# The first 30 microseconds of a gated dilated convolution: who writes the zeros, when the second x is asked for, and the order of the first octet

## The chip, the cores and the metric

The kernel runs on one core of a Trainium2 chip. The metric is device time in microseconds (us), as the median of a few runs. Beside it stands one profiled execution, from which all rows below are taken; the profile names the engines PE (TensorE matmul), PEld (TensorE weight load), DVE (VectorE), ACT (ScalarE), POOL (GpSimd) and SP (SyncE). A name with a q behind it (SPq, ACTq) is the engine's own sequencer, on which it issues DMAs.

## The reference

```
B, T, D, K = 2, 16000, 144, 15          # all bf16; x (B,T,D), w (K,D,2D), w_o (D,D)
xp = pad(x, 28 rows of zeros ahead of each sequence)
h  = sum over i of  xp[:, 28-2i : 28-2i+T, :] @ w[i]       # a causal convolution, dilation 2
z  = tanh(h[..., :D]) * sigmoid(h[..., D:])
return z @ w_o
```

So each output row needs 15 input rows two apart, each times a 144x288 matrix, then a gate and a 144x144 product.

## The kernel before

**Tiling.** Each of the two sequences is cut into 8 windows of 2048 rows with 32 rows ahead (16 windows in all). Within a window the rows are taken by their index modulo 16: one matmul has 128 rows, 16 apart, as its stationary operand. The 8 even or 8 odd residues of a window form an *octet*; there are 32 octets. The convolution is not computed tap by tap. The 15 taps are combined by sums of weights and differences of inputs in the manner of a fast filter algorithm, so that each octet needs fewer products. The sums of weights are made once, on VectorE (`sm`, `ss`, `a1v`, `av`, `ev`, part of `bc`) and on TensorE by products with an identity (`raw_sums`, `pair_sums`, into `bcv` and `bc`; ScalarE copies them out). The differences of x (`d2`, `d4`, `d8`, `d28`, `d24`, `d48`, `d248`) are made by VectorE for each window.

**The 128 + 16 split of the channels.** The 144 channels are 128 plus 16. The 128 come in by a transposing DMA straight from x (`xn`, line 89). The other 16 take a detour. `gather` loads them to `xt` (line 99; 104 partitions of 22 pieces of 32 bytes). ScalarE copies them by residue (`rest`, line 113), VectorE forms a difference (`rest_diff`, line 117), and `spread` (line 123) writes both halves, of 104x4 pieces of 160 bytes each, to a DRAM scratch `xg`. `remainder` (line 128) then reads `xg` back by transposing DMAs, as `rx` (first half) and `re` (second half). Rows of `xg` that lie ahead of a sequence, or past its end, are written with zeros or with rows of x (lines 217 to 229).

**The order of the work.** All engines but GpSimd are scheduled by hand: instructions run on each engine in the order in which the program issues them. Each DMA takes one of a few semaphores in turn and waits until the last user of that semaphore has landed. SP's queue holds the loads of x and of w, the raw remainder weights (lines 205, 206), `rx`, `re`, then the next window's `xt` and `xn`, and so on. From the first octet on, the order comes from `PLAN` (line 16), a list of named steps, each with an offset in octets; they are sorted into `todo` (line 556) and issued one by one (line 568). Pieces of the first octet's preparation are put before a named step by `late` (line 301).

**The named steps.** An octet has leaves A1, A2, A3, B, C, E. `v` is a leaf's common matmuls, `k` a ScalarE copy of that bank, `p` its private matmuls, `d` a ScalarE duplicate of a bank, `B2`, `B3`, `C2` direct matmuls with `d24` and `re`. `q`, `t3` and `y` are VectorE combinations that read those banks and so free them. A2 and A3 need `rx`; B2, B3, C2 and E need `re`. `xl` loads a window's x, `xt` its 16 other channels, `cr` and `dr` are `rest` and `rest_diff`, `wg` is `spread`. There are five PSUM banks for B, C and E, two for A and one (`po`) for the output product.

**Ahead of it all**, 20 matmuls of zeros (128x512, line 186) run on TensorE while the first loads come in.

**Out-projection weights.** `wo_z`, `wo_m` and `wo_bd` hold w_o in shifted copies (lines 248 to 259): 16 loads for `wo_z`, one for `wo_m`, 8 for `wo_bd`, all issued by GpSimd. `wo_z` is first used by the output product of octet 0 (line 440), three octets later; the other two serve only the last octet.

Of the kernel before, what the change touches and what calls it, by code (L numbers as in the profile page):

```python
# [8 lines left out]
BF16 = mybir.dt.bfloat16  # L9
F32 = mybir.dt.float32  # L10
# [16 lines left out]
def kernel(  # L27
# [14 lines left out]
    nc = tc.nc  # L42
    P = 128
    NWARM = 20
    MANUAL = {mybir.EngineType.PE, mybir.EngineType.Activation, mybir.EngineType.DVE, mybir.EngineType.SP}
    B, T, D = x.shape
    K = w.shape[0]
    D2 = w.shape[2]
    assert D2 == 2 * D and w.shape[1] == D and D == 144 and K == 15
    CM = 128  # L50
    CR = D - CM
    NG = 8
    H = 32
    WT = 16 * P
    WB = H + WT
    NJ = WB // 4 + 8
# [3 lines left out]
    wins = []  # L60
# [55 lines left out]

        nc.vector.tensor_tensor(out=sets[wi]["xs"][:, 1], in0=by_residue(wi, 2), in1=by_residue(wi, 0), op=ALU.subtract)

    def spread(wi, eng=nc.sync):

        for q in (0, 1):
            dst = bass.AP(xg.tensor, xg[wi, q, H // 4 * (wins[wi][1] == 0), 0:1].offset, [[5 * CR, NX], [NJ * CR, 4], [1, 5 * CR]])
            eng.dma_start(out=dst, in_=sets[wi]["xs"][:, q].rearrange("p r j c -> p r (j c)"))

# [41 lines left out]
    def add(o, a, b_, eng=None):  # L166
        (eng or nc.vector).tensor_tensor(out=o, in0=a, in1=b_, op=ALU.add)
# [34 lines left out]
    nc.gpsimd.memset(raw[96:P, 1, :], 0.0)  # L202
    for c in range(0, 16, 4):
        nc.sync.dma_start(out=w_all[:, c:min(c + 4, K), :], in_=w[c:min(c + 4, K), 0:CM, :].rearrange("k c d -> c k d"))  # L204
    nc.sync.dma_start(out=raw[:, 0, :], in_=w[0:K:2, CM:D, :])
    nc.sync.dma_start(out=raw[0:P - CR, 1, :], in_=w[1:K:2, CM:D, :])


    swap = const.tile([P, P], BF16)
    nc.gpsimd.memset(swap[:], 0.0)  # L210
# [1 line left out]
                            compare_op=ALU.not_equal, fill=1.0, base=CR - P, pattern=[[CR, NG], [-1, CR]], channel_multiplier=1)  # L212
    ident = const.tile([P, P], BF16)
    make_identity(nc, ident[:])


    nc.scalar.dma_start(out=xg[:].rearrange("w q n c -> (w q) (n c)")[:, 4 * NJ * CR:], in_=zero[0:2 * NW, 0:CR * CR])
    for wi in [i for i in range(NW) if wins[i][1] == 0]:
        def ahead_of(q, r, n, j, rows):
            return bass.AP(xg.tensor, xg[wi, q, r * NJ + j, 0:1].offset, [[NJ * CR, n], [1, rows * CR]])  # L220
        eng = nc.gpsimd if wi else nc.scalar
        eng.dma_start(out=ahead_of(0, 0, 4, 0, H // 4), in_=zero[0:4, 0:H // 4 * CR])
        eng.dma_start(out=ahead_of(1, 0, 2, 0, H // 4), in_=zero[0:2, 0:H // 4 * CR])
        eng.dma_start(out=ahead_of(1, 2, 2, 0, H // 4 - 1), in_=zero[0:2, 0:H // 4 * CR - CR])
        eng.dma_start(out=ahead_of(1, 2, 2, H // 4 - 1, 1), in_=x[wins[wi][0], 0:2, CM:D])
    for lo, e in [(i + 1, i + NW // B) for i in range(0, NW, NW // B)]:
        for q in (0, 1):
            dst = bass.AP(xg.tensor, xg[lo, q, WB // 4, 0:1].offset, [[2 * (4 * NJ + 16) * CR, e - lo], [NJ * CR, 4], [1, H // 4 * CR]])
            nc.gpsimd.dma_start(out=dst, in_=zero[0:4 * (e - lo), 0:H // 4 * CR])
    rest(0)  # L230

    s_r = const.tile([P, D2], BF16)
# [2 lines left out]
    def summed(parts, outs):  # L235

        t = bank(False)
        for i, (l, r) in enumerate(parts):
            nc.tensor.matmul(t[:, 0:D2], lhsT=l, rhs=r, start=i == 0, stop=i == len(parts) - 1)
        for o, sign in outs:  # L240
            nc.scalar.mul(out=o, in_=t[:, 0:D2], mul=sign)

    def rest_sums(which):
        even, odd = ((swap[:], raw[:, k, :]) for k in (0, 1))
        for parts, outs in (([even, odd], [(s_r[:], 1.0), (ns_r[:], -1.0)]), ([odd], [(wo_p[:], 1.0)]), ([even], [(we_r[:], 1.0)]))[which]:
            summed(parts, outs)

    nc.gpsimd.dma_start(out=wo_m[:], in_=w_o[0:CM, :])

    nc.gpsimd.memset(wo_z[:], 0.0)  # L250
    for g in range(9):
        if g:
            nc.gpsimd.dma_start(out=wo_z[0:CR * g, g, 0, :], in_=w_o[D - CR * g:D, :])
        if g < 8:
            nc.gpsimd.dma_start(out=wo_z[CR * g:P, g, 1, :], in_=w_o[0:P - CR * g, :])

    nc.gpsimd.memset(wo_bd[:], 0.0)
    for g in range(NG):
        nc.gpsimd.dma_start(out=wo_bd[g * CR:(g + 1) * CR, g, :], in_=w_o[CM:D, :])
    pre0 = derive_steps(sets[0])  # L260
    for k in ("d8", "d4"):
        pre0[k]()
    rest_diff(0)
    spread(0, nc.scalar)
    remainder(0, 0)
    remainder(0, 1)

# [13 lines left out]
        if c == 2:  # L281
            pre0["d48"]()

    def raw_sums(j):
        for e in (1, 0):
            summed([(ident[:], w_all[:, 8 * j + 2 * i + e, :]) for i in range(4)], [(bcv[:, j, e], 1.0)])

    bc = const.tile([CM, 4, 2, D2], BF16, name="bc")

    def pair_sums(j):  # L290
        for i in (2 * j, 2 * j + 1):
            for e in (1, 0):
                summed([(ident[:], wq[:, i, k, e, :]) for k in (0, 1)], [(bc[:, i, e, :], 1.0)])

    raw_sums(0)
    pair_sums(0)
    add(av[:], quad[:, :, 0], quad[:, :, 1])
    pre0["d2"]()
    add(bc[:, 2:4], wq[:, 2:4, 0], wq[:, 2:4, 1])
    pre0["d28"]()  # L300
    late = [(0, {"pA1_0"}, lambda: rest_sums(slice(0, 3))), (0, {"pA2_0", "vB", "vC"}, lambda: raw_sums(1)), 
            (0, {"q2_0", "B2_0", "B2_1", "C2_0", "C2_1", "vE"}, lambda: pre0["d24"](slice(0, 1))),
            (0, {"q3_0", "B3_0", "B3_1", "vE"}, lambda: pre0["d24"](slice(1, 2))),
            (0, {"q3_0", "B3_0", "B3_1", "vE"}, lambda: add(ev[:], w_all[:, 0:16:8, :], w_all[:, 4:16:8, :])),
            (0, {"yB2_0", "pE_0"}, pre0["d248"])]

    def mm(ps, l, r, start, stop, on=False):
        nc.tensor.matmul(ps[:, 0:D2], lhsT=l, rhs=r, start=start, stop=stop, skip_group_check=on)  # L308

# [154 lines left out]
    def issue(n, name):  # L464
        wi, rho = octs[n]
        if name == "xl":
            sets[wi].update(load(wi))
            sets[wi].update(steps=derive_steps(sets[wi]))
            return
        s = sets[wi]  # L470
        if name in fetch:
            fetch[name](wi)
            return
        if name in s["steps"]:
            s["steps"][name]()
            return
        if n not in live:
            live[n] = Octet(s, rho)
            live[n].by_phase = n == NO - 1
        o = live[n]  # L480
        if name[0] in "vkpd" and name[1] in "ABCE":
            leaf = getattr(o, name[1:3] if name[1] == "A" else name[1] + "1")
            if name[0] == "v":
                leaf.common()
            elif name[0] == "k":
                leaf.copy()
            else:
                (leaf.private if name[0] == "p" else leaf.dup)(int(name[-1]))
        elif name[:2] == "t3":
            o.t3(int(name[-1]))  # L490
        elif name[:3] == "a1s":
            o.a1s(int(name[-1]))
        elif name[0] == "q":
            o.q(*((o.A2, "q2") if name[1] == "2" else (o.A3, "q3")), int(name[-1]),
                ALU.subtract if name[1] == "2" else ALU.add)
        elif name[0] in "BC":
            getattr(o, name[0:2])(int(name[-1]))
        elif name[0] == "y":
            leaf = {"B": o.B1, "C": o.C1, "E": o.E1}["E" if name[1:3] == "C3" else name[1]]
            ts, q = (leaf.other, "q3") if name[1:3] == "B3" else (leaf.ts, "t3" if name[1:3] == "C3" else "q2")  # L500
            k = (0 if name[1] == "B" else 1) + (2 if name[2] == "3" else 0)
            o.out_y(k, ts, q, ALU.subtract if name[1] == "B" else ALU.add, int(name[-1]))
        elif name[:2] == "th":
            o.act(int(name[2]), "th", 0, ACT.Tanh)
        elif name[:2] == "sg":
            o.act(int(name[2]), "sg", D, ACT.Sigmoid)
        elif name[0] == "m":
            for part in "ab" if o.by_phase else "z":
                o.mult(int(name[1]), part)
        elif name == "zt":  # L510
            o.zt = z_load(o.t["z"])
        elif name[0] == "g":
            outproj(o, int(name[1]))
        elif name[:2] == "po":
            project_out(o, window_out(n), int(name[2]))
        else:
            assert name == "ost"
            store(wi, nc.scalar)
# [16 lines left out]
    def finish():  # L535
# [11 lines left out]
        for g, by in ((0, "ACT"), (1, "DVE"), (2, "ACT")):  # L547
# [5 lines left out]
    even = set(pre0) | set(fetch) | {"xl"}  # L553
    outwards = {"g0", "g1", "g2", "po0", "po1", "po2", "ost"}
    at_wg = next((at, i) for i, (name, at) in enumerate(plan) if name == "wg")
    todo = sorted((2 + at_wg[0], False, at_wg[1] - .5, n, name) if n == 2 and name in ("cr", "dr") else
                  (n + at, n > 1 and n + at < 0, i, n, name) for i, (name, at) in enumerate(plan) for n in range(NO)
                  if not (name in even and (n % 2 or n == 0) or name == "ost" and n % 2 == 0
                          or name in outwards and n >= NO - 3 or name == "zt" and n == NO - 1))
    gates = [(NO - 1, "m1")]  # L560
    for *_, n, name in todo:
        for e in [e for e in late if n == e[0] and name in e[1]]:
            e[2]()
            late.remove(e)
        if (n, name) in gates:
            gates.clear()
            finish_early()
        issue(n, name)
# [29 lines left out]
```

## Time and profile before

| | us |
|---|---|
| median of 3 runs (335.77 to 337.07) | 336.16 |
| the profiled execution, its own time | 338.06 |
| its span, first to last instruction | 336.3 |
| end of the 20 matmuls of zeros | 7.2 |
| first matmul with x (leaf A1 of octet 0) | 11.48 |
| first matmul with `rx` | 18.39 |
| first matmul with `re` | 21.38 |
| start of TensorE's last wait in the front, and its end | 25.09, 27.58 |
| first output product (`po`) | 45.54 |
| last matmul | 331.05 |

The busy table gives each engine's busy time over the span; the chain of waits follows the end of the kernel back to what released each step; the timeline lists instructions in order of time, with the idle time ahead of them and its releaser in brackets; the table of stretches gives each engine's busy time in one microsecond, with TensorE's granted clock (1.00 is full speed) and what the DMA engines moved. From the start to landing, DMAs of POOL took between 2.7 and 5.9 us; for the DMAs of SP and ACT the trace has no landing time of their own, and it is read from the instruction that waited for them.

### The profile page before, as it was taken

The page shows a single profiled execution, that of the slowest core. Times are in us where ns is not written, and L with a number is a line of the kernel's source. Part 1 is how long each engine was busy: PE and PEld are TensorE (multiplying, and loading weights), DVE is VectorE, ACT ScalarE, POOL GpSimd, SP SyncE. Part 2 cuts the span into 40 slices and gives each one's busy share as a digit, 9 for nine tenths or more (in the row PEclk, how much of TensorE's full clock was granted, in tenths as well). Part 3 has the DMA queues.
Part 4 walks back from the last instruction along what each step waited for, and adds up shares of the span by engine and source line. Part 5 has one row for each costly group of instructions (what it writes and reads, how often), then busy time and mean ns, then how long its engine had stood idle before and what let it go on. Part 6 is the DMA issues. An engine that isn't in the chain of part 4 may idle for free.

```text
span 336.3 us, 7414 instructions
## 1 busy us (share of the span) xinstructions
PE 322.1 (96%) x2649; PEld 303.3 (90%) x2649; DVE 293.9 (87%) x664; ACT 241.6 (72%) x571; POOL 22.7 (7%) x49
## 2 busy tenths in 40 slices
PE   7597999999999999999999999999999999999993
PEld 2485999999999999999999999999999999999982
DVE  2848999999989999999989999998989999998683
ACT  2542778877777787777777787777777887777763
POOL 7980000000000000000000000000000000000000
PEclk9897999999999999999999999999999999999999
DMA  9996558495976859595996858596885949484313
GB/s 168 170 153 122 132 101 190 111 196 144 162 185 119 187 108 209 115 187 161 119 226 115 174 115 198 130 167 177 119 209 111 202 98 230 122 140 131 37 35 127
DMA packets 195282, 49.64 MB, mean 148 GB/s; under 512 B 190786, under 2 KB 193198, under 8 KB 195246
## 3 DMA queue, kind: packets, MB, share of 16 engines
q1 hardware_dynamic: 188894, 40.07, 65.0%
q10 hardware_dynamic: 5296, 8.67, 7.4%
q0 software_dynamic: 1056, 0.44, 0.6%
q8 instruction: 20, 0.33, 0.4%
q14 instruction: 16, 0.13, 0.1%
HBM read 2.82 MB, written 11.40 MB: 42 GB/s over the span
## 4 chain that ended last, share of the span: by engine, by line
PE 89%; DMA 5%; SPq 2%; DVE 1%; issue 1%; ACT 0%; DVEq 0%; ACTq 0%
PE bc L308 55%; PE a L308 25%; PE po L440 9%; DMA xn<-in_x_dram 2%; DMA w_all<-in_w_dram 2%; SPq L128 2%; DMA xg<-xs 1%; SPq L89 0%; DVE o L432 0%; DVE y L398 0%; DVE z L410 0%; PE bc L444 0%; SPq L204 0%; SPq L99 0%; PE bc L447 0%
## 5 line engine op out<-in xcount | busy, mean ns | idle before, releaser
L308 PEld LDWEIGHTS <-d 128*128 128x128 bf16 x1792 | 226.0, 145 | 10.7 <-issue 3.5
L308 PE MATMUL bc<-w_all,d 128*128 128x288 bf16 x832 | 140.6, 287 | 0.3 <-DVE t L393 0.3
L398 DVE TENSOR_TENSOR y<-q,bc 128x288 f32<-128x288 f32 x192 | 86.5, 451 | 8.0 <-PE bc L308 6.0
L337 ACT COPY bc<-bc 128x288 f32<-128x288 f32 x97 | 38.5, 397 | 34.2 <-PE bc L308 29.1
L375 DVE TENSOR_TENSOR q<-a1s,a 128x288 f32<-128x288 f32 x126 | 54.3, 454 | 1.9 <-PE a L308 1.1
L430 ACT CAST o<-po 128x432 bf16<-128x432 f32 (+1 forms) x87 | 41.6, 478 | 17.0 <-PE po L440 17.0
L160 DVE TENSOR_TENSOR d<-d 128x516 bf16<-128x516 bf16 (+3 forms) x65 | 52.3, 806 | 0.0
L308 PE MATMUL a<-sm,d 128*128 128x288 bf16 x252 | 50.8, 289 | 0.0
L160 DVE TENSOR_TENSOR d<-xn 128x516 bf16<-128x516 bf16 (+2 forms) x48 | 41.3, 863 | 8.3 <-DMA xn<-in_x_dram 8.3
L337 ACT COPY a<-a 128x288 f32<-128x288 f32 x95 | 36.7, 386 | 12.2 <-PE a L308 9.0
L403 ACT ACTIVATE th<-y 128x576 bf16<-128x576 f32 x64 | 43.8, 684 | 1.1 <-DVE y L398 1.1
L403 ACT ACTIVATE sg<-y 128x576 bf16<-128x576 f32 x64 | 43.7, 682 | 0.0
L440 PE MATMUL po<-wo_z,zt 128*128 128x144 bf16 (+1 forms) x323 | 43.4, 253 | 0.0
L308 PE MATMUL bc<-bc,d 128*128 128x288 bf16 x256 | 41.8, 286 | 0.2 <-ACT bc L337 0.2
L308 PE MATMUL bc<-we_r,re 128*128 128x288 bf16 x128 | 36.9, 288 | 0.0
L308 PE MATMUL bc<-wo_p,re 128*128 128x288 bf16 x128 | 36.6, 286 | 0.0
L393 DVE TENSOR_TENSOR t<-q,bc 128x288 f32<-128x288 f32 x64 | 28.8, 451 | 8.3 <-PE bc L308 8.3
L440 PEld LDWEIGHTS <-zt 128*128 128x128 bf16 x341 | 29.9, 98 | 4.1
L341 ACT COPY bc<-bc 128x288 f32<-128x288 f32 x64 | 24.9, 391 | 11.7 <-PE bc L308 11.6
L398 DVE TENSOR_TENSOR y<-t,bc 128x288 f32<-128x288 f32 x64 | 26.3, 455 | 6.2 <-PE bc L308 6.2
L308 PEld LDWEIGHTS <-re 128*128 128x128 bf16 x256 | 28.9, 113 | 0.1
L410 DVE TENSOR_TENSOR z<-th,sg 128x576 bf16<-128x576 bf16 (+1 forms) x66 | 29.0, 442 | 0.0
(74 smaller groups left out, 270.2 us busy)
## 6 DMA issues: line engine op xcount, KB each, us to landing
out_dram<-o ACTq DMA_DIRECT2D x13, 576.0 KB
xg<-xs SPq DMA_DIRECT2D x30, 65.0 KB
xt<-in_x_dram SPq DMA_DIRECT2D x13, 71.5 KB
w_all<-in_w_dram SPq DMA_DIRECT2D x3, 288.0 KB
out_dram<-o SPq DMA_DIRECT2D x1, 576.0 KB
zt<-z SPq DMA_TRANSPOSE x31
out_dram<-o ACTq DMA_DIRECT2D x1, 468.0 KB
out_dram<-o ACTq DMA_DIRECT2D x1, 288.0 KB
```

The lines of the kernel that those rows point to most:

```text
L128: nc.sync.dma_start_transpose(out=t[:], in_=bass.AP(xg.tensor, xg[wi, q, 0:1, 0:1].offset, [[CR, 4 * NJ], [1, P]]))
L160: nc.vector.tensor_tensor(out=o, in0=a, in1=b_, op=ALU.subtract)
L308: nc.tensor.matmul(ps[:, 0:D2], lhsT=l, rhs=r, start=start, stop=stop, skip_group_check=on)
L337: nc.scalar.copy(out=self.ts[1][:, 0:D2], in_=self.ts[0][:, 0:D2])
L341: nc.scalar.copy(out=self.other[i][:, 0:D2], in_=self.ts[i][:, 0:D2])
L375: nc.vector.tensor_tensor(out=self.get(cp_pool, name, [P, 2, D2], F32)[:, i, :], in0=self.t["a1s"][:, i, :], in1=leaf.ts[i][:, 0:D2], op=op)
L393: nc.vector.tensor_tensor(out=self.get(cp_pool, "t3", [P, 2, D2], F32)[:, i, :], in0=self.t["q3"][:, i, :], in1=self.C1.ts[i][:, 0:D2], op ...
L398: nc.vector.tensor_tensor(out=y[:, k + 4 * i, :], in0=self.t[q][:, i, :], in1=ts[i][:, 0:D2], op=op)
L403: nc.scalar.activation(out=t[:], in_=self.t["y"][:, k::2, lo:lo + D], func=func)
L410: nc.vector.tensor_tensor(out=o, in0=th[:, :, lo:lo + n], in1=sg[:, :, lo:lo + n], op=ALU.mult)
L430: nc.scalar.copy(out=o, in_=a)
L440: nc.tensor.matmul(o.po[g][:, (a - r0) * D:(e - r0) * D], lhsT=o.zt[:, c, :], rhs=wo_z[:, c, a - c + 1:e - c + 1, :].rearrange("p r e -> p ...
```

## The change

In words, in the order of the program:

- The two raw remainder loads (lines 205, 206) are issued by SP behind the second of the four loads of w instead of behind the fourth.
- The zeros at the end of `xg`, and those of window 0, are issued by GpSimd instead of ScalarE. Those of the other windows are issued behind window 0's spread, by GpSimd as before.
- Window 0's spread is split: the first half is issued by ScalarE, the second by GpSimd (`engines` in `spread`).
- The out-projection weights are cleared and loaded later: `weights_out` is called behind the sum `ev`, and a one-element copy of `ev` on GpSimd (`held`) holds the loads until that sum is done. `wo_m` comes behind `wo_z`.
- `rest_sums` (four matmuls with `raw`) runs behind `raw_sums(0)`, ahead of the pair sums; `raw_sums(1)` is split in two, one half ahead of octet 0's first step and one behind it.
- `keep(n)` issues n matmuls of zeros (128x512) into the `po` bank: 5, 1 and 2 at three places of the front.
- The load of the second window's x (`xl` of octet 2) is issued on SP right behind `re`, ahead of that window's `xt`.
- Octet 0's steps up to `yB2_0` and `d248` are listed in `first`; what is listed is left out of `todo`'s run. `late` is gone.
- GpSimd joins the engines scheduled by hand.

```diff
-    MANUAL = {mybir.EngineType.PE, mybir.EngineType.Activation, mybir.EngineType.DVE, mybir.EngineType.SP}
+    MANUAL = {mybir.EngineType.PE, mybir.EngineType.Activation, mybir.EngineType.DVE, mybir.EngineType.SP, mybir.EngineType.Pool}
...
-    def spread(wi, eng=nc.sync):
+    def spread(wi, engines=(nc.sync, nc.sync)):
-        for q in (0, 1):
+        for q, eng in enumerate(engines):
...
     for c in range(0, 16, 4):
         nc.sync.dma_start(out=w_all[:, c:min(c + 4, K), :], in_=w[c:min(c + 4, K), 0:CM, :].rearrange("k c d -> c k d"))
-    nc.sync.dma_start(out=raw[:, 0, :], in_=w[0:K:2, CM:D, :])
-    nc.sync.dma_start(out=raw[0:P - CR, 1, :], in_=w[1:K:2, CM:D, :])
+        if c == 4:
+            nc.sync.dma_start(out=raw[:, 0, :], in_=w[0:K:2, CM:D, :])
+            nc.sync.dma_start(out=raw[0:P - CR, 1, :], in_=w[1:K:2, CM:D, :])
+    def ahead_of(wi):
...
+        nc.gpsimd.dma_start(out=rows(0, 0, 4, 0, H // 4), in_=zero[0:4, 0:H // 4 * CR])
+        nc.gpsimd.dma_start(out=rows(1, 0, 2, 0, H // 4), in_=zero[0:2, 0:H // 4 * CR])
+        nc.gpsimd.dma_start(out=rows(1, 2, 2, 0, H // 4 - 1), in_=zero[0:2, 0:H // 4 * CR - CR])
+        nc.gpsimd.dma_start(out=rows(1, 2, 2, H // 4 - 1, 1), in_=x[wins[wi][0], 0:2, CM:D])
...
-    nc.scalar.dma_start(out=xg[:].rearrange("w q n c -> (w q) (n c)")[:, 4 * NJ * CR:], in_=zero[0:2 * NW, 0:CR * CR])
-    for wi in [i for i in range(NW) if wins[i][1] == 0]:
...
-        eng = nc.gpsimd if wi else nc.scalar
...
+    nc.gpsimd.dma_start(out=xg[:].rearrange("w q n c -> (w q) (n c)")[:, 4 * NJ * CR:], in_=zero[0:2 * NW, 0:CR * CR])
+    ahead_of(0)
     rest(0)
...
-    spread(0, nc.scalar)
+    spread(0, (nc.scalar, nc.gpsimd))
+    for wi in [i for i in range(1, NW) if wins[i][1] == 0]:
+        ahead_of(wi)
...
+    def keep(n):
+        t = ps_o.tile([P, 512], F32, name="po", tag="po")
+        for _ in range(n):
+            nc.tensor.matmul(t[:], lhsT=zero[:, 0:P], rhs=zero[:], start=True, stop=True)
     raw_sums(0)
+    rest_sums(slice(0, 3))
     pair_sums(0)
+    pair_sums(1)
+    keep(5)
+    raw_sums(1, (1,))
     add(av[:], quad[:, :, 0], quad[:, :, 1])
     pre0["d2"]()
     add(bc[:, 2:4], wq[:, 2:4, 0], wq[:, 2:4, 1])
     pre0["d28"]()
-    late = [(0, {"pA1_0"}, lambda: rest_sums(slice(0, 3))), (0, {"pA2_0", "vB", "vC"}, lambda: raw_sums(1)), 
...
+    pre0["d24"](slice(0, 1))
...
+    def weights_out():
+        nc.gpsimd.memset(wo_z[:], 0.0)
+        nc.gpsimd.memset(wo_bd[:], 0.0)
+        held = const.tile([1, 1], BF16)
+        nc.gpsimd.tensor_copy(out=held[:], in_=ev[0:1, 0, 0:1])
...
+    def evs():
+        add(ev[:], w_all[:, 0:16:8, :], w_all[:, 4:16:8, :])
+        weights_out()
+    first = ["vA1", "kA1", lambda: raw_sums(1, (0,)), lambda: keep(1), "pA1_0", "pA1_1", "a1s_0", "a1s_1", "vA2", "kA2", lambda: keep(2), "vB",
+             "kB", "pA2_0", "q2_0", "pA2_1", "q2_1", "vA3", "kA3", "pB_0", "dB_0", "pB_1", "dB_1", lambda: pre0["d24"](slice(1, 2)), "pA3_0",
+             "q3_0", "pA3_1", "B2_0", "q3_1", "B2_1", evs, "yB2_0", pre0["d248"]]
+    late2 = [(2, "xl")]
+    for n, name in late2:
+        issue(n, name)
+    for f in first:
+        f() if callable(f) else issue(0, f)
...
     for *_, n, name in todo:
-        for e in [e for e in late if n == e[0] and name in e[1]]:
-            e[2]()
-            late.remove(e)
+        if (n, name) in done:
+            continue
```

More of the change, by code (lines that the diff above doesn't have):

```diff
@@ L204, with rows @@
         nc.sync.dma_start(out=w_all[:, c:min(c + 4, K), :], in_=w[c:min(c + 4, K), 0:CM, :].rearrange("k c d -> c k d"))
-    nc.sync.dma_start(out=raw[:, 0, :], in_=w[0:K:2, CM:D, :])
-    nc.sync.dma_start(out=raw[0:P - CR, 1, :], in_=w[1:K:2, CM:D, :])
+        if c == 4:
+            nc.sync.dma_start(out=raw[:, 0, :], in_=w[0:K:2, CM:D, :])
+            nc.sync.dma_start(out=raw[0:P - CR, 1, :], in_=w[1:K:2, CM:D, :])
+    def ahead_of(wi):
+        def rows(q, r, n, j, k):
+            return bass.AP(xg.tensor, xg[wi, q, r * NJ + j, 0:1].offset, [[NJ * CR, n], [1, k * CR]])
+        nc.gpsimd.dma_start(out=rows(0, 0, 4, 0, H // 4), in_=zero[0:4, 0:H // 4 * CR])
+        nc.gpsimd.dma_start(out=rows(1, 0, 2, 0, H // 4), in_=zero[0:2, 0:H // 4 * CR])
+        nc.gpsimd.dma_start(out=rows(1, 2, 2, 0, H // 4 - 1), in_=zero[0:2, 0:H // 4 * CR - CR])
+        nc.gpsimd.dma_start(out=rows(1, 2, 2, H // 4 - 1, 1), in_=x[wins[wi][0], 0:2, CM:D])
     swap = const.tile([P, P], BF16)
@@ L214 @@
     make_identity(nc, ident[:])
-    nc.scalar.dma_start(out=xg[:].rearrange("w q n c -> (w q) (n c)")[:, 4 * NJ * CR:], in_=zero[0:2 * NW, 0:CR * CR])
-    for wi in [i for i in range(NW) if wins[i][1] == 0]:
-        def ahead_of(q, r, n, j, rows):
-            return bass.AP(xg.tensor, xg[wi, q, r * NJ + j, 0:1].offset, [[NJ * CR, n], [1, rows * CR]])
-        eng = nc.gpsimd if wi else nc.scalar
[L222 to L229, printed above, removed]
+    nc.gpsimd.dma_start(out=xg[:].rearrange("w q n c -> (w q) (n c)")[:, 4 * NJ * CR:], in_=zero[0:2 * NW, 0:CR * CR])
+    ahead_of(0)
     rest(0)
@@ L246, in rest_sums @@
             summed(parts, outs)
[L248 to L259, printed above, removed]
     pre0 = derive_steps(sets[0])
@@ L263 @@
     rest_diff(0)
-    spread(0, nc.scalar)
+    spread(0, (nc.scalar, nc.gpsimd))
+    for wi in [i for i in range(1, NW) if wins[i][1] == 0]:
+        ahead_of(wi)
+    for lo, e in [(i + 1, i + NW // B) for i in range(0, NW, NW // B)]:
+        for q in (0, 1):
+            dst = bass.AP(xg.tensor, xg[lo, q, WB // 4, 0:1].offset, [[2 * (4 * NJ + 16) * CR, e - lo], [NJ * CR, 4], [1, H // 4 * CR]])
+            nc.gpsimd.dma_start(out=dst, in_=zero[0:4 * (e - lo), 0:H // 4 * CR])
     remainder(0, 0)
@@ L282, with raw_sums, pair_sums @@
             pre0["d48"]()
-    def raw_sums(j):
-        for e in (1, 0):
+    def raw_sums(j, es=(1, 0)):
+        for e in es:
             summed([(ident[:], w_all[:, 8 * j + 2 * i + e, :]) for i in range(4)], [(bcv[:, j, e], 1.0)])
     bc = const.tile([CM, 4, 2, D2], BF16, name="bc")
[L290 to L293, printed above, removed]
+    def pair_sums(i):
+        for e in (1, 0):
+            summed([(ident[:], wq[:, i, k, e, :]) for k in (0, 1)], [(bc[:, i, e, :], 1.0)])
+    def keep(n):
+        t = ps_o.tile([P, 512], F32, name="po", tag="po")
+        for _ in range(n):
+            nc.tensor.matmul(t[:], lhsT=zero[:, 0:P], rhs=zero[:], start=True, stop=True)
     raw_sums(0)
+    rest_sums(slice(0, 3))
     pair_sums(0)
+    pair_sums(1)
+    keep(5)
+    raw_sums(1, (1,))
     add(av[:], quad[:, :, 0], quad[:, :, 1])
@@ L300 @@
     pre0["d28"]()
-    late = [(0, {"pA1_0"}, lambda: rest_sums(slice(0, 3))), (0, {"pA2_0", "vB", "vC"}, lambda: raw_sums(1)),
[L302 to L305, printed above, removed]
+    pre0["d24"](slice(0, 1))
     def mm(ps, l, r, start, stop, on=False):
@@ L555 @@
     at_wg = next((at, i) for i, (name, at) in enumerate(plan) if name == "wg")
+    def weights_out():
[3 more added lines that the diff above has]
+        nc.gpsimd.tensor_copy(out=held[:], in_=ev[0:1, 0, 0:1])
+        for g in range(9):
+            if g:
+                nc.gpsimd.dma_start(out=wo_z[0:CR * g, g, 0, :], in_=w_o[D - CR * g:D, :])
+            if g < 8:
+                nc.gpsimd.dma_start(out=wo_z[CR * g:P, g, 1, :], in_=w_o[0:P - CR * g, :])
+        nc.gpsimd.dma_start(out=wo_m[:], in_=w_o[0:CM, :])
+        for g in range(NG):
+            nc.gpsimd.dma_start(out=wo_bd[g * CR:(g + 1) * CR, g, :], in_=w_o[CM:D, :])
+    def evs():
[9 more added lines that the diff above has]
+        f() if callable(f) else issue(0, f)
+    done = [(0, f) for f in first if not callable(f)] + late2 + [(0, "d24"), (0, "d248")]
     todo = sorted((2 + at_wg[0], False, at_wg[1] - .5, n, name) if n == 2 and name in ("cr", "dr") else
```

## The prediction

> **What bounds the kernel.** I read the busy table first, then the waits of the first 32 us, then the chain that ended last, then a table of stretches of one microsecond, and last the timeline of 6 to 47 us.
>
> ```profile
> PE 322.1 (96%) x2649; PEld 303.3 (90%) x2649; DVE 293.9 (87%) x664; ACT 241.6 (72%) x571; POOL 22.7 (7%) x49
> ```
>
> ```profile
> 27.58 0.41 PE L308 MATMUL bc<-ev,d 128*128 128x288 bf16 x2 [2.49 <-DVE y L398]
> ```
>
> TensorE is busy 96% of the span, and from 27.58 us to 323 us its timeline has no gap worth naming. So the end is set by the moment V at which it starts that unbroken run (27.58, the matmul of ev and d24 in octet 0), and by what it does afterwards. The change touches only what lies before V, so the question is: how much sooner is V, and does TensorE keep its pace behind it?
>
> ```profile
> 8.75 3.26 DMA xg<-xs
> 12.02 2.27 SPq L128
> 14.40 3.01 SPq L128
> 17.46 0.55 SPq L99
> 18.07 7.59 DMA xn<-in_x_dram
> ...
> 26.85 0.32 DVE xs L117
> 27.17 0.37 DVE y L398
> 27.58 1.48 PE bc L308 x7
> ```
>
> This is the chain in order of time. V waits for the y of line 398, which frees its bank. VectorE takes that y in program order behind d2 of the second window and behind the difference xs, and d2 waits for the second x (window 1's xn) until 25.66. That transpose is issued by SP at 18.07, behind xt (17.46), the transposes re (14.40) and rx (12.02), and rx waits for the spread of xs into xg (8.75, landed 12.01). The engine that stands still is TensorE, but the path is SP's queue.
>
> ```profile
> 13.00:14.00 1.00, 0.29 (x2) 0.10 (x1) 1.00 (x2) 0.38 (x1) 1.00 (x3) 1.00 0.89 193
> 16.00:17.00 1.00, 1.00 (x6) 0.64 (x5) 0.54 (x1) 0.93 (x3) 1.00 (x3) 0.50 1.52 132
> 20.00:21.00 1.00, 1.00 (x10) 0.98 (x9) 0.77 (x3) 0.73 (x3) 0.85 (x2) 1.00 1.62 50
> 26.00:27.00 1.00, 0.00 (x0) 0.00 (x0) 1.00 (x2) 0.00 (x0) 0.00 (x0) 1.00 0.25 44
> 29.00:30.00 1.00, 1.00 (x6) 0.65 (x5) 0.70 (x3) 0.34 (x1) 0.00 (x0) 0.50 1.08 61
> ```
>
> Columns: stretch, length, busy time of PE, PEld, DVE, ACT, POOL, granted clock, DMA share, GB/s. Twice TensorE stands mostly idle (11 to 14 and 25 to 27.5), and each time some 3.3 us at half clock follow (14.75 to 18.1, 28.4 to 31.7).
>
> **The change, part by part.** Times are of the profiled execution (338.06 us, 336.3 of it the span); the median shown is 1.90 less, and I take the same saving off it.
>
> (1) *Zeros by GpSimd, rx.* Before, ACT issues five writes to xg (1.84 to 7.33) before it copies xs (7.37), and its spread then waits until 8.75 for a reused semaphore. After, only the xt load stands ahead of the copy. xt had landed by 6.58 at the latest (the write of line 225 waits for its semaphore and starts 0.07 behind its predecessor). So: 6.58 + 0.05 + 0.46 (copy) + 0.05 + 3.26 (landing, as before) = 10.4 instead of 12.01. The zeros that rx needs go out from GpSimd at 2.5 and 3.2 and land in 4.8 to 5.9 (the four L222 to L225 rows): 9.1 at most. rx issues 10.4 to 12.7 (12.02 to 14.29 before).
>
> (2) *The second half of the spread goes by GpSimd.* VectorE's difference ends at 7.73 as before, behind xn's landing. re waits for this transfer. No row has GpSimd write 416 pieces of 160 B: its rows have 2 to 128 pieces and cost 0.48 to 0.68 of issue, with no slope between 16 and 128 pieces, and land after 2.7 to 5.9. Bounds 10.5 and 13.7; I take the zeros' middle, 5.4, as they ran while the DMA engines were as full: 13.2. re starts at 13.2 instead of 14.40: **-1.2**.
>
> (3) *re's issue* took 3.01; the next re (31.14) took 1.95. Its slow part is a stretch at 84 to 89 GB/s with wo_z loads about, which now come later. I take 2.5, ends 15.7: **-0.5**.
>
> (4) *xt behind the second x*: 0.55 + 0.06 leave SP's path: **-0.6**. The second x starts at 15.8.
>
> (5) *Its issue* took 3.69, the third one (33.18) 2.07. Between 19.5 and 21 the DMA moved 34 to 98 GB/s: those are xt's 2,288 pieces of 32 B ahead of it in the same queue. rx at 28.10, again behind an xt, took 2.93 against 1.9 later. So 2.1, bound 3.69: **-1.6**. End of issue 17.9, landing 3.9 later as before (25.66 less 21.76; rx 4.1): 21.8. The four terms are 3.9.
>
> (6) *xt itself* now starts at 18.0. Landing bounds: not before the x ahead of it (21.8), not over 5.7 after issue (the first xt, 0.91 to 6.58 at most): 23.7. The middle, 22.75, is hidden behind d2 (21.8 + 1.16 = 22.96); at the upper end V moves by 0.7. V = 22.96 + 0.73 (26.85 to 27.58) = 23.7.
>
> (7) *Is TensorE there by then?* The list of octet 0 and the eight products of zeros (0.215 each at full clock, 1.7 together) cost nothing only under cover. From 8.7 to the first use of rx it has 38 products of 0.123 (4.7), the 1.7 and its short waits: about 15.1, while rx lands at 12.7 + 4.1 = 16.8. Then 16 products (2.0) to the first use of re, 18.8, against re's landing at 15.7 + 3.9 = 19.6. Then 30 products (3.7): 23.3, against V = 23.7. So all are covered, the last by 0.4 only; without cover the zeros cost 1.7. w_all's fourth load waits for xn's landing (6.27) instead of the first load's (7.51), and has 135 KB of raw ahead (about 0.5 us at 290 GB/s): not later than 11.69.
>
> (8) *The clock behind V.* The second half-clock stretch costs 17 products 0.12 each, 2.0 at most. But VectorE is nearly full there: from 27.08 to 36.92 its timeline has only 0.92 of idle time. Bounds 0 and 0.92; I take half: **-0.5**. [...]
>
> (9) *Out-projection weights* start behind ev, near 20: 16 loads of wo_z by 0.54 plus 4.6 to land end at 33.2; their first use is 45.54 less 4.4. wo_m and wo_bd serve the last octet. Cost 0, with 8 us of cover.
>
> (10) *Late next*: rx of window 1. Its spread starts behind xt (22.75 + 0.5), lands 3.17 later, then 2.93 and 4.1: 33.5, needed at 39.05 less 4.4 = 34.65. Covered by 1.
>
> Sum: 3.9 + 0.5 = 4.4. **336.16 - 4.4 = 331.8.**
>
> **Rivals.** (A) *xt becomes the wait in the second x's place*, because its small pieces come last. The 1.5 us they took, started at x's end of data (19.7) and with 3.9 to land, gives 25.1; V = 25.8, saving 1.8: 334.4. For it: DMA rows at 34 to 98 GB/s; against: the first xt landed within 5.7 beside other loads. Chance 0.14. (B) *The DMA engines, not the queue, set the landing*: the second x comes 1.5 sooner at most: 334.7. For it: shares above 1.2 from 14 to 23; against: 0.34 to 0.69 at 11 to 13.5, and 0.07 from 23.5 on. Chance 0.15. (C) *GpSimd's spread is late and the kernel slower.* If its price goes by pieces, or its work stands behind VectorE's, it lands late; SP then sits on re with the second x, xt and the second spread queued behind it. Break-even is 25.66 less 3.9, 2.1, 0.1 and 2.5: re at 17.1, 9.3 after the difference, when the longest GpSimd row is 5.9. At twice 5.4, 10.8, re starts at 18.6 and the end is 337.7. Against it: GpSimd's issues between 11.8 and 16.5 took 0.51 to 0.58 with VectorE full. Chance 0.06. [...] (D) *Nothing is gained*, as TensorE's new order is itself late (the 0.4 of cover in step 7 and the zeros' 1.7): 335.8. Chance 0.05.
>
> **From these to the numbers.** The forecast has 0.60: 331.8, in itself 329.8 (re at 12.0, issues of 1.95, all of the 0.92) to 333.8 (re at 13.7, issues in between). A and B stretch the range to 334.9; C and D, and the upper tail of B, are left out. A measurement here tells about 0.5% (1.7 us) from no change. Faster by more: 0.60, 0.10 of A and 0.08 of B, 0.78. Within: 0.04 of A, 0.07 of B and 0.04 of D, 0.15. Slower: C and the rest of D, 0.07.
>
> **What would show it.** In the new profile: ACT's xs copy by 6.6 and rx's issue by 10.4 (1); re's issue at 13.2 (2); the second x issued near 15.8 in about 2.1 and d2 starting near 21.8 (4, 5); the difference xs not waiting for xt (6); TensorE's wait at the ev product below 1 us, and a granted clock of 1.00 from 8 us on (7, 8); no wait at the first po (9). I am wrong if re starts after 15, if the second x takes 7 us again, if xs waits for xt, or if TensorE drops to half clock around 24.

## The result and the profile after

The kernel after takes 332.75 us in the median (332.49 to 334.28, 6 runs), beside 336.62 for the kernel before on the same chip (335.20 to 337.95, 6 runs): a ratio of 0.9896, 95% interval 0.9862 to 0.9930. Forecast were 331.8, with a range of 329.8 to 334.9. The profiled execution took 332.82 us, 330.8 of it the span.

From here on V is, as in the prediction, the start of the matmul of `ev` and `d24` in octet 0, behind which TensorE runs without a gap worth naming. It came at 27.58 in the profile before; here is the chain of waits of the kernel after (start, length, what):

```profile
12.57 1.19 SPq L128
...
13.93 2.33 SPq L128
...
16.30 2.07 SPq L89
...
18.41 4.40 DMA xt<-in_x_dram
...
23.08 0.46 DVE y L392
...
23.58 1.14 PE bc L302 x7
```

The first row is the rest of `rx`'s issue (11.64 to 13.76), the next are the issues of `re` and of the second x. Put this beside the chain of before: the 7.59 us of the second x's transfer (`xn`) have gone from it, and another transfer stands in its place, `xt`, 4.40 long. V moved from 27.58 to 23.58. The timeline of the kernel after shows how close the race is:

```profile
16.63 0.31 PE L302 MATMUL bc<-ns_r,rx 128*128 128x288 bf16 x1 [0.66 <-DMA rx<-xg]
...
20.73 1.24 DVE L160 TENSOR_TENSOR d<-xn 128x2078 bf16<-128x2078 bf16 x1
...
22.84 0.32 DVE L117 TENSOR_TENSOR xs<-xt 104x320 bf16<-104x320 bf16 x1 [0.86 <-DMA xt<-in_x_dram]
...
23.58 0.41 PE L302 MATMUL bc<-ev,d 128*128 128x288 bf16 x2 [0.66 <-DVE y L392]
```

The second row has no bracket: `d2` of the second window started when VectorE was free, so the second x had landed by 20.73, where before it came at 25.66. The third row has one: `xs` waited 0.86 us for `xt`, and the y behind it held TensorE for 0.66. The stretches of one microsecond (length, then busy time of PE, PEld, DVE, ACT and POOL, granted clock, DMA share, GB/s):

```profile
16.00:17.00 1.00, 0.37 (x3) 0.37 (x4) 0.55 (x1) 0.12 (x1) 0.27 (x1) 1.00 1.23 274
...
20.00:21.00 1.00, 1.00 (x10) 0.99 (x9) 1.00 (x3) 0.00 (x0) 0.62 (x2) 1.00 0.97 69
...
26.00:27.00 1.00, 1.00 (x10) 0.99 (x9) 1.00 (x3) 0.59 (x2) 1.00 (x3) 1.00 1.10 94
```

The granted clock is 1.00 in each of them, where before it was 0.50 at 16 and at 29 to 31. The slow moment of the DMA engines, 69 GB/s at a share of 0.97, is still there in the second row (`xt`'s small pieces), but the second x is no longer behind it. TensorE's wait of 2.49 ahead of V has become one of 0.66; the other wait in the timeline above, also 0.66, is for `rx`.

**Where the time came from.** V sets the end. From the start of V's matmul to the start of the last matmul it is 301.8 to 302.0 us in ten of the fourteen profiles of this study. It is 303.5 in the three in which half clock follows V (before, before_again, xt_first), and 302.6 in zeros_act, which has a wait behind V. In the profiled pair the last matmul came 5.45 sooner (325.60 instead of 331.05): 4.0 are V's move, and 1.45 are the clock.

For the medians the split is an estimate. A half-clock stretch of 3.3 us lowers the mean clock of a span by about 3.3 / 336 / 2 = 0.005. So the mean clock tells how much half clock an execution had. The 55 executions of the kernel before that ran beside the experiments differ in this:

| mean granted clock | half clock, in stretches of 3.3 us | executions | mean span, us |
|---|---|---|---|
| 0.997 to 0.999 | 0 | 9 | 333.97 |
| 0.990 to 0.994 | 1 | 21 | 334.69 |
| 0.987 to 0.989 | 2 | 17 | 335.46 |
| 0.980 to 0.985 | 3 | 8 | 335.66 |

Not all of this half clock costs time. In all fourteen profiles the clock also falls behind the last matmul, 1.0 to 4.3 us after its end, where no matmul is left to slow. The profile of before_keep has a mean clock of 0.994, and this is its only half clock (its last matmul starts at 328.11, its span ends at 333.3):

```profile
330.00:331.00 1.00, 0.00 (x0) 0.00 (x0) 0.00 (x0) 0.00 (x0) 0.00 (x0) 0.50 1.06 286
```

The median span of the 55 is 334.9. The six executions of the kernel after have spans of 330.2 to 330.8, in the median 330.45, and mean clocks of 0.995 to 0.999. The nine executions of the first row have hardly any half clock, so 333.97 - 330.45 = 3.5 us is an estimate of V's move, and 334.9 - 333.97 = 0.9 one of the clock. 0.5 is lost again outside the span (2.3 us lie around it after, 1.8 before; why is not known): 3.9 in the medians. The profiled execution of the kernel before, with its span of 336.3, was a long one: only 4 of the 55 are as long.

### The profile page after: what moved, and what is told of

Its sections match the earlier page's. It is cut to its first block, busy times and chain, and to the rows that moved or that the text cites. A ratio compares the mean times of both kernels' runs of the same rounds, so it can differ in the third digit from the quotient of the medians.

```text
span 330.8 us, 7432 instructions
## 1 busy us (share of the span) xinstructions
PE 321.4 (97%) x2657; PEld 303.1 (92%) x2657; DVE 293.5 (89%) x664; ACT 242.0 (73%) x571; POOL 26.3 (8%) x56
## 4 chain that ended last, share of the span: by engine, by line
PE 90%; DMA 4%; SPq 2%; DVE 2%; issue 1%; POOL 1%; ACT 0%; DVEq 0%
PE bc L302 56%; PE a L302 25%; PE po L434 9%; DMA xn<-in_x_dram 2%; DMA xt<-in_x_dram 1%; SPq L128 1%; DMA xg<-zero 1%; SPq L89 1%; DVE d L160 0%; DVE o L426 0%; DVE y L392 0%; DVE z L404 0%; POOL xg L123 0%; PE bc L438 0%; PE bc L441 0%
## 5 line engine op out<-in xcount | busy, mean ns | idle before, releaser
L434 PEld LDWEIGHTS <-zt 128*128 128x128 bf16 x341 | 29.9, 98 | 4.1
```

The costliest lines, as they stand in the source:

```text
L434: nc.tensor.matmul(o.po[g][:, (a - r0) * D:(e - r0) * D], lhsT=o.zt[:, c, :], rhs=wo_z[:, c, a - c + 1:e - c + 1, :].rearrange("p r e -> p ...
```

## The experiments

V is read from each kernel's one profile; ratios are to runs of the kernel before on the same chip, with 95% intervals. The profiles of list_alone and before_keep fell on the shortest of their ten executions (spans of 333.2 and 333.3), so V is early in them.

| kernel | median us | ratio | median span | second x issued, took | V | TensorE's wait at V |
|---|---|---|---|---|---|---|
| after | 332.75 | 0.9896 (0.9862 to 0.9930) | 330.45 | 16.30, 2.07 | 23.58 | 0.66 |
| queue_alone | 332.24 | 0.9854 (0.9811 to 0.9897) | 330.3 | 15.82, 2.06 | 23.37 | 0.37 |
| list_alone | 337.41 | 1.0018 (0.9993 to 1.0043) | 335.0 | 16.42, 3.72 | 25.99 | 2.57 |
| before_keep | 336.23 | 0.9985 (0.9962 to 1.0009) | 334.35 | 16.64, 3.78 | 26.19 | 0.57 |
| after_nokeep | 332.27 | 0.9843 (0.9808 to 0.9879) | 330.15 | 15.85, 2.18 | 22.94 | 0.43 |
| xt_first | 335.95 | 0.9975 (0.9948 to 1.0001) | 334.05 | 16.51, 3.10 | 25.38 | 2.75 |
| zeros_act | 333.69 | 0.9918 (0.9889 to 0.9946) | 331.5 | 15.97, 2.13 | 23.72 | none |
| spread_act | 332.53 | 0.9885 (0.9839 to 0.9930) | 330.6 | 15.61, 1.93 | 22.93 | 0.95 |
| weights_free | 333.22 | 0.9900 (0.9846 to 0.9954) | 331.35 | 16.29, 2.10 | 24.55 | 1.68 |
| xt_early_sp | 331.86 | 0.9849 (0.9822 to 0.9877) | 329.5 | 15.73, 2.19 | 22.34 | none |
| xt_pool | 332.06 | 0.9853 (0.9828 to 0.9878) | 330.2 | 16.35, 2.04 | 23.34 | none |
| queue_xt | 331.83 | 0.9855 (0.9824 to 0.9887) | 329.8 | 16.34, 1.96 | 23.11 | none |

The theory was that V is set on SP's queue by the second x, and that asking for it sooner and ahead of `xt` is what the change is worth. Rivals: that TensorE's new order carries it, that the products of zeros carry it through the clock, or that the moves of the zeros, the spread and the weights do.

**One half at a time: queue_alone and list_alone.** The first is the kernel before with what the change does to transfers (zeros and half of the spread by GpSimd, weights behind `ev`, `xl` of octet 2 ahead of `xt`); octet 0 keeps its old order, the raw loads their old place, and there are no products of zeros. The second is the kernel after with those transfers put back.

```diff
 # queue_alone, on the kernel before
+    spread(0, (nc.scalar, nc.gpsimd))
...
+    issue(2, "xl")
     for *_, n, name in todo:
+        if (n, name) == (2, "xl"):
+            continue
```

> The kernel before with the transfers' half of the change alone: zeros and the second half of the spread by GpSimd, out-projection weights behind ev, second x ahead of xt; TensorE's order, the raw loads' place and the products of zeros as before. Theory (SP's queue sets V): rx issues near 11.6, the second x near 16.3, the difference xs waits for xt near 22.8, V within 0.5 of 23.6, so 3.5 to 5 us saved. Rival (TensorE's new order and the zeros do it): V stays above 26 and the time within 1.5 us of before.

> The changed kernel with the transfers' half undone: zeros and both halves of the spread by ScalarE, weights loaded early, xt ahead of the second x; TensorE's new order, the early raw loads and the products of zeros stay. Theory: V stays at 27 to 28, because the second x still lands near 25.7; the first half-clock stretch may go, without a gain; time within 1 us of before. Rival (order and zeros do it): 3 us or more saved.

The timelines of V, of queue_alone and then of list_alone:

```profile
22.63 0.32 DVE L117 TENSOR_TENSOR xs<-xt 104x320 bf16<-104x320 bf16 x1 [0.94 <-DMA xt<-in_x_dram]
...
23.37 0.41 PE L318 MATMUL bc<-ev,d 128*128 128x288 bf16 x2 [0.37 <-DVE y L408]
```

```profile
24.09 1.24 DVE L160 TENSOR_TENSOR d<-xn 128x2078 bf16<-128x2078 bf16 x1 [2.48 <-DMA xn<-in_x_dram]
...
25.99 0.41 PE L311 MATMUL bc<-ev,d 128*128 128x288 bf16 x2 [2.57 <-DVE y L401]
```

queue_alone has the whole gain, and its wait is the same one for `xt`. list_alone has none of it in the median (its V of 25.99, ahead of the 27 to 28 expected, is that of its shortest execution): TensorE's part is done by 23.42 instead of 25.09, and it stands 2.57 us before the same late x. The new order of octet 0, the earlier raw loads and the products of zeros are worth nothing here by themselves, and nothing that can be told on top of the transfers.

**The order of two loads: xt_first.** The kernel after, with `xt` ahead of the second x again.

```diff
-    late2 = [(2, "xl")]
+    late2 = [(2, "xt"), (2, "xl")]
```

> The changed kernel with the next xt put ahead of the second x again, all else kept. Theory: xt's 0.55 of issue and its 2,288 small pieces slow the transpose behind it; its issue takes 3.5 or more instead of 2.07, d2 waits for x near 23.5, xs no longer waits for xt, V near 25.2, about 1.6 us of the saving lost. Rival (the order of these two does not matter, the last of them lands at the same time either way): V within 0.4 of 23.6.

Two views of it, the timeline and the stretches:

```profile
15.91 0.56 SPq L99 DMA_DIRECT2D xt<-in_x_dram  x1
16.51 3.10 SPq L89 DMA_TRANSPOSE xn<-in_x_dram  x1
...
23.49 1.24 DVE L160 TENSOR_TENSOR d<-xn 128x2078 bf16<-128x2078 bf16 x1 [3.03 <-DMA xn<-in_x_dram]
...
25.38 0.41 PE L302 MATMUL bc<-ev,d 128*128 128x288 bf16 x2 [2.75 <-DVE y L392]
```

```profile
18.00:19.00 1.00, 1.00 (x10) 0.89 (x9) 0.84 (x3) 0.32 (x2) 0.00 (x0) 1.00 1.29 49
...
27.00:28.00 1.00, 1.00 (x6) 0.69 (x5) 1.00 (x4) 0.14 (x1) 1.00 (x3) 0.50 1.15 99
```

The x is asked for at nearly the same time as in the kernel after (16.51 against 16.30), but its issue takes 3.10 instead of 2.07, and it lands at 23.49 instead of by 20.73. In between the DMA engines are busy (1.29) and move 49 GB/s: the 2,288 pieces of 32 bytes go first. V is 1.80 later, and with the long wait the half clock is back (26.5 to 29.9). Of its ten executions the two with a clock of 0.997 have a span of 332.25, 1.8 above the kernel after, like V; the other eight have 333.6 to 335.4. So the order of this one pair of issues holds 3.6 of the 4.45 us of median span, over twice the 1.6 expected: about half by V and half by the clock (1.8 and 1.5 in the two profiles).

**The products of zeros: after_nokeep and before_keep.** The first takes all eight out of the kernel after, the second puts ten into the wait of the kernel before.

```diff
 # after_nokeep: "keep(5)", "lambda: keep(1)" and "lambda: keep(2)" taken out
 # before_keep, on the kernel before
+            (0, {"vE"}, lambda: keep(10))
```

> The changed kernel without its eight products of zeros. Theory: they lie under the wait for rx; without them the matmuls ahead of rx end earlier and wait longer, V stays at 23.6 and the time within 0.5 us, as long as no 3.3 us stretch is mostly idle. Rival (they hold the clock): half clock appears between 12 and 20 and V moves by 1 us or more.

> The kernel before with ten products of zeros ahead of the ev product, in TensorE's wait at 25.1. This measures what the half clock behind V costs. Clock theory: V stays at 27.6, the clock stays at 1.00 there, and the time from V to the first output product falls from 17.96 to about 16.4, 1.5 us saved. Rival (VectorE is full there, as the prediction had it): 0.5 us or less saved though the clock stays full.

Without them the kernel after is as fast (span 330.15), and its clock stays at 1.00 over waits of 0.63 and 0.43. Ahead of the first half clock of before TensorE was mostly idle for four microseconds (10 to 14, busy 0.12 to 0.53 of each); here only single microseconds are as idle (0.31 at 8, 0.38 at 12). Half clock also came after less, a wait of 2.32 (before_again). In before_keep the ten products fill 2.32 us of the wait; its profile has no half clock behind V, and from V to the first output product it takes 16.4, as the kernel after does (16.45), against 17.96 before. But its time, 0.7 us less, is not told from that of before, and neither the 1.5 us of the clock theory nor its rival is shown. The mean clocks of its executions, 0.989 to 0.997, do not help, as they count the half clock behind the last matmul too. How often the zeros keep the clock up in a long wait stays open; the change needs none, as the longest wait it leaves at V or for `rx` is 0.66 (0.63 in after_nokeep).

**The kernel before once more: before_again.** Unchanged.

> The kernel before, a second look. The runs beside the experiments have spans of 333.6 to 337.1 for it, and the execution that the prediction was made against 336.3. Theory: that execution was a slow one, with rx at 12.02 and the second x at 18.07; in another V is near 26.2 (as in the kernel before with ten products of zeros), and the saving in V is nearer 2.7 than 4.0. Rival: V is 27.6 again.

337.41 us, span 335.6. The second x was issued at 17.41 (3.73 long), landed at 25.06, V was 26.95, TensorE waited 2.32, and half clock followed from 27.6 to 31; V to the first output product 17.96, as before. The mechanism is that of the first profile; V is 0.6 sooner, not the 1.4 that the theory had. Against this profile V's move is 3.4.

**Who writes the zeros: zeros_act.** The kernel after with window 0's zeros issued by ScalarE again.

```diff
-    nc.gpsimd.dma_start(out=xg[:].rearrange("w q n c -> (w q) (n c)")[:, 4 * NJ * CR:], ...)
-    ahead_of(0)
+    nc.scalar.dma_start(out=xg[:].rearrange("w q n c -> (w q) (n c)")[:, 4 * NJ * CR:], ...)
+    ahead_of(0, nc.scalar)
```

> The changed kernel with window 0's zeros and the end rows written by ScalarE again, ahead of its copy of xs. Theory: the copy of xs moves from 6.7 to about 7.4 and the spread behind it, so rx issues 0.5 to 1 us later and V moves by as much. Rival (rx is released by something else, such as the DMA engines being full of w): rx's issue does not move.

```profile
8.32 0.46 ACT L113 COPY xs<-xt 104x320 bf16<-104x320 bf16 x1 [6.07 <-DMA raw<-in_w_dram]
...
12.48 0.46 DVE L167 TENSOR_TENSOR sm<-w_all 128x576 bf16<-128x576 bf16 x1 [2.85 <-DMA w_all<-in_w_dram]
...
15.00 0.28 PE L302 MATMUL a<-a1v,xn 128*128 128x288 bf16 x1 [1.29 <-DVE a1v L167]
```

ScalarE's copy is 1.61 later than in the kernel after (6.71), but `rx` is issued at 11.63, not later (11.64). So the rival held. What is lost is elsewhere: DMAs take their semaphores in turn, so SP's second raw load waits 2.4 for `xt` to land and its two last loads of w 1.5 more for a write of zeros. They are issued from 9.05 on instead of 5.13. The sums of weights come later, and TensorE itself becomes the bound: it reaches V at 23.72 with no wait. The median span is 331.5, 1.05 above the kernel after, though the intervals of the two ratios overlap. Only 0.14 of that is V; in the profile TensorE waits another 0.46 behind V, at 34.24, for the second window's `rx`.

**Who spreads, and when the weights come: spread_act and weights_free.**

```diff
 # spread_act
-    spread(0, (nc.scalar, nc.gpsimd))
+    spread(0, (nc.scalar, nc.scalar))
 # weights_free: no wait for ev, issued ahead of the second x
-        held = const.tile([1, 1], BF16)
-        nc.gpsimd.tensor_copy(out=held[:], in_=ev[0:1, 0, 0:1])
...
+    weights_out()
     late2 = [(2, "xl")]
```

> The changed kernel with both halves of the spread issued by ScalarE. Theory: re then waits for the second half about as long as now (it landed 4.1 us after GpSimd's issue at 7.9), since ScalarE issues it near 8 and has no copies out of PSUM due before 9; V within 0.4 of 23.6. Rival C (GpSimd's share of the spread matters): re starts earlier by 0.5 us or more.

> The changed kernel without the one-element copy that holds the out-projection weights: their loads start behind GpSimd's memsets, near 16.5 instead of 20.5, beside re, the second x and xt. Theory: 25 loads are 2 us of DMA time at most; re and the second x land up to 0.5 us later, V within 0.7 of 23.6. Rival (their removal is what made the front faster): V moves by 1.5 us or more.

spread_act is like the kernel after (span 330.6, V 22.93); its `d2` waited 0.75 for the second x, until 20.57, which dates that landing: 3.0 behind the end of the issue. In weights_free the loads of `wo_z` run from 16.0, beside the second x. Its timeline and one of its stretches:

```profile
22.10 1.24 DVE L160 TENSOR_TENSOR d<-xn 128x2078 bf16<-128x2078 bf16 x1 [1.39 <-DMA xn<-in_x_dram]
```

```profile
21.00:22.00 1.00, 1.00 (x11) 0.99 (x9) 0.00 (x0) 0.77 (x3) 0.60 (x2) 1.00 1.58 32
```

The x has the same issue (16.29, 2.10 long) but lands 1.4 later at least, and V is 0.97 later; the span is 0.9 longer, though the intervals of the two ratios overlap. So holding the weights back seems to help, and as the issue is no longer, by clearing the DMA engines rather than SP's queue. The parts do not add up: the order of the two loads (3.6), the zeros (1.05) and the weights (0.9) are more than 4.45 together, as each was taken out with the others in place.

**The last wait taken away: xt_early_sp, xt_pool and queue_xt.** The kernel after waits for `xt`. xt_early_sp lets SP issue it early, behind the loads of w (6.46); xt_pool lets GpSimd issue it behind its half of the spread (8.91); queue_xt is queue_alone with the early `xt` of the first.

```diff
 # xt_early_sp, on the kernel after; queue_xt has the same on queue_alone
+    gather(1)
     def ahead_of(wi):
...
-    done = [...] + late2 + [(0, "d24"), (0, "d248")]
+    done = [...] + late2 + [(0, "d24"), (0, "d248"), (2, "xt")]
 # xt_pool: behind the spread
     spread(0, (nc.scalar, nc.gpsimd))
+    gather(1, nc.gpsimd)
```

> The changed kernel with window 1's xt loaded by SP right behind the loads of w (near 6.6), while SP waits for the spread. Theory: xs no longer waits for xt, which landed at 22.81 and set V; V is then TensorE's own arrival, 22.9, 0.6 us sooner, if the 2,288 pieces, now among the last loads of w, do not hold the spread and rx up by more. Rival: they do, rx issues 1 us or more later and V is 24 or later.

> The changed kernel with window 1's xt loaded by GpSimd behind its half of the spread (issue near 8.8), so that its pieces fall into the stretch at 11 to 13 in which the DMA engines moved 7 to 15 GB/s. Theory: as above, V near 22.9, 0.6 us saved, and rx unmoved. Rival: GpSimd's price grows with the pieces (0.85 for the spread's 416 against 0.50), about 3 us for 2,288, the zeros behind it come late, and the next window's rx waits for them.

> This is the transfers' half of the change alone (octet 0 listed as in the kernel before, no products of zeros, raw behind the second half of w), with window 1's xt issued by SP early, behind the loads of w. Theory (with xt out of the way the last thing in front of V is TensorE's own arrival, and the list of octet 0 with the earlier raw is what brings it there sooner): in queue_alone xs waited 0.94 for xt and TensorE then 0.37 for y, so V comes 0.37 sooner at most, near 23.0, with no wait of TensorE, against 22.34 with the list (xt_early_sp): time near 332.2, some 0.3 to 0.6 above xt_early_sp. Rival (the list is worth nothing here either): V at 22.3 to 22.5 and the same time as xt_early_sp, 331.9. Second rival: xt early holds up rx and re here, V at 23.4 or later and 332.3 or more.

The timeline of xt_early_sp:

```profile
21.37 0.32 DVE L117 TENSOR_TENSOR xs<-xt 104x320 bf16<-104x320 bf16 x1
...
22.34 0.41 PE L304 MATMUL bc<-ev,d 128*128 128x288 bf16 x2
```

Neither row has a bracket: with `xt` out of the way TensorE reaches V by its own work, at 22.34 (22.9 expected), and the span falls by about 1 us, to 329.5. In queue_xt it reaches V at 23.11, also with no wait, as its theory had it: there the list of octet 0 and the earlier raw loads are worth 0.8 of V, and 0.3 of span, which the times do not tell (331.83 and 331.86). In xt_pool V is at 23.34, as `rx` comes later for TensorE (17.22, with a wait of 1.13). xt_early_sp and queue_xt have the shortest spans of the study and stand clearly below the kernel before, but the intervals of their ratios overlap that of the kernel after.

## Why the prediction was right, and where its terms were not

The mechanism was right: the path was SP's queue, and the second x asked for sooner, ahead of `xt`, is what moved V. The total held (4.4 forecast, 3.9 measured in the medians), and so did V's move (3.9 forecast; 4.0 in the profiled pair, about 3.5 in the medians). But several terms were off and cancelled, and that is luck. One of the four signs of being wrong came true as well: `xs` waited for `xt`.

- *Step 1, rx at 10.4: failed.* The copy was in time (6.71), and so was the spread's issue (7.20), but `rx` was issued at 11.64: the write took 4.4 to land, not the 3.26 that I had from one later write. In the fourteen profiles, writes issued at 6.8 to 7.5 held `rx` for 4.1 to 5.0 us and those issued at 8.2 to 8.8 for 2.2 to 3.3, so that `rx` was issued between 10.9 and 12.0 either way. An earlier write bought nothing (zeros_act); what holds the early ones was not tested.
- *Step 2, re at 13.2 behind GpSimd's write: failed in its reason.* `re` was issued at 13.93. It waited for `rx`'s issue to end (13.76), not for GpSimd, whose write landed 4.1 after its issue instead of 5.4. The gain was 0.5 instead of 1.2. GpSimd's part is free, but not needed either (spread_act).
- *Step 3, 0.5: right* (0.7); the issue took 2.33. *Step 4, 0.6: right.*
- *Step 5: issue right, landing not.* 2.07 was measured, 2.1 forecast. But the landing, at 20.73 or sooner, was 2.4 behind the end of issue at most (3.0 in spread_act), not 3.9 as before. The old 3.9 held the same cause as the long issue, the small pieces ahead: it is 3.9 again in xt_first, where `wo_z` starts only at 20.15. Loads of `wo_z` beside the x lengthen it too (3.7 in weights_free); how the old 3.9 divides between the two was not measured. I took the cause off the issue and left it in the landing. This error made up for steps 1 and 2.
- *Step 6, xt hidden: failed.* `xt` landed at 22.81, the middle of my bounds (22.75). But `d2` ended 1 us sooner than forecast, and so `xt` was the last. This is the mechanism of rival A, at a price of 0.66 of V instead of 2.1. V came at 23.58 against 23.7.
- *Step 7: right.* TensorE was at V by 22.92 (23.3 forecast), and the zeros cost nothing that the times tell (after_nokeep). They gain nothing either.
- *Step 8, the clock, 0.5 with bounds of 0 and 0.92: mis-sized.* In the profiled pair it is 1.51 (from V to the first output product 17.96 before, 16.45 after), in the medians about 0.9 by the estimate above. The upper bound was wrong. I had summed VectorE's idle times in the timeline and called the engine full. Its rows overlap; here are some of the kernel before, and then the same ones of the kernel after:

```profile
29.15 0.45 DVE L398 TENSOR_TENSOR y<-q,bc 128x288 f32<-128x288 f32 x1
29.89 0.46 DVE L375 TENSOR_TENSOR q<-a1s,a 128x288 f32<-128x288 f32 x1 [0.30 <-PE a L308]
...
36.92 0.46 DVE L398 TENSOR_TENSOR y<-q,bc 128x288 f32<-128x288 f32 x1 [0.23 <-PE bc L308]
```

```profile
25.15 0.45 DVE L392 TENSOR_TENSOR y<-q,bc 128x288 f32<-128x288 f32 x1
25.51 0.45 DVE L369 TENSOR_TENSOR q<-a1s,a 128x288 f32<-128x288 f32 x1
...
31.41 0.45 DVE L392 TENSOR_TENSOR y<-q,bc 128x288 f32<-128x288 f32 x1
```

  At full clock a row of 0.45 is followed by the next after 0.36 (25.15 to 25.51). At half clock the gap from start to start is 0.74, of which the bracket shows 0.30 as idle; really 0.38 were lost. From the first y (27.08 and 23.08) to the last row shown, the same work takes 9.84 before and 8.33 after: VectorE had 1.51 to give.
- *Step 9, the weights at no cost: right* (no wait at the first output product). That their move also clears the second x's way, by nearly 1 us of V (weights_free), stood nowhere in the sum. *Step 10: right*; the next `rx` was issued at 25.67 and TensorE waited for nothing there.

Of the rivals, B (the DMA engines set the landing) would have had the second x at 24.2; it came by 20.73. C (GpSimd late) fails, as GpSimd's write landed at 12.0, ahead of the end of `rx`'s issue, and spread_act without it is no faster. D has nothing for it in the profile: TensorE was early and waited 0.66.

## What to carry to other kernels

Where two loads stand in one queue, look at which one's reader comes first and at their pieces: in xt_first a load of 2,288 small pieces took 0.56 us to issue, and the x queued behind it landed at 23.49, where ahead of it (kernel after) it was there by 20.73. Put behind the x, that load left a wait of 0.66 at V; put early, at 6.46, while the queue stood idle, it left none (xt_early_sp). These are the two places to try. When the wait at the end of a path is removed, time the second-latest arrival just as carefully, from rows that do not share the disturbance that goes away. And do not read slack from a sum of idle brackets where records overlap: compare how long the same list of rows takes from first start to last start.

## What the runs showed of the hardware

- **Small pieces ahead of a transposing DMA in its queue lengthened it twice.** In xt_first, list_alone, before_keep and before_again the transpose of the second x behind an `xt` of 2,288 pieces of 32 bytes took 3.10 to 3.78 us to issue and landed 3.9 us behind the end of that. Where the x went first or `xt` was issued long before, in nine kernels, the issue took 1.93 to 2.19, and the x landed 3.0 behind it in spread_act and 2.4 at most in the kernel after (3.7 in weights_free, with loads of `wo_z` beside it). While the small pieces went, the DMA engines were busy and moved little: in one microsecond between 18 and 21, shares of 0.97 to 1.64 and 47 to 69 GB/s (before, before_again, list_alone, xt_first and the kernel after). The pieces are not the only cause of a long issue: the third x of the kernel after, issued at 30.88 with its `xt` 6.7 us ahead of it, took 3.34.
- **Half clock followed a wait of 2.32 us, and did not follow one of 2.57.** At V it came after waits of 2.32 (before_again), 2.49 (before) and 2.75 us (xt_first), and not after 2.57 (list_alone) or 1.68 (weights_free). It began 0.6 to 1.1 us after TensorE had resumed, and lasted 3.4. Behind the last matmul it began 1.0 to 4.3 us after its end (4.1 in before and after). So one profile does not tell the clock's part of the median; what sets the moment was not shown.
- **GpSimd's issue grew far less than the pieces**: 0.48 to 0.68 us for up to 128, 0.85 to 0.99 for 416, 1.42 for 2,288 (xt_pool, where a rival had 3).
